# Four sums of a chunk's transform as adding transfers between on-chip tiles

## The chip, the cores and the metric

The kernel runs on one core of one Trainium2 chip. The metric is the device time of one execution in microseconds (us). TensorE multiplies matrices into PSUM banks; VectorE (DVE), ScalarE (ACT) and GpSimd (POOL) work on tiles in SBUF; SyncE (SP) issues the transfers (DMAs), which run on 16 engines that all queues share. Each engine works through its own list of instructions in order and waits on semaphores for the others.

## The reference

Two layers, each a Fourier mixing of a [2048, 512] activation followed by a token-shift and MLP block:

```
def _A_ref(x, dft_seq_re, dft_seq_im, dft_hid_re, dft_hid_im):
    a = jnp.einsum("bsd,ed->bse", x, dft_hid_re)
    b = jnp.einsum("bsd,ed->bse", x, dft_hid_im)
    y = jnp.einsum("ts,bse->bte", dft_seq_re, a) - jnp.einsum("ts,bse->bte", dft_seq_im, b)
    return y
...
x = x + _A_ref(_layernorm(x), ...)
x = x + _B_ref(_layernorm(x), w1, w2, w3, w4)
x = x + _A_ref(_layernorm(x), ...)
x = x + _B_ref(_layernorm(x), w1, w2, w3, w4)
```

`_B_ref` is a layer norm, a product with `w1`, a gelu, shifts of a quarter of the columns by one or two rows, a product with `w2` and a residual, then a second layer norm and an MLP of width 1376. Only the Fourier mixing is touched by the change.

## The kernel before

**Precision.** Every fp32 product is made of three: a matrix is held as a high part, which is its cast to the type `float32r`, and a low part, the rest. `mm3` (lines 294 to 296) issues high x high, high x low and low x high. So each tile that TensorE is to read needs two steps first: a cast on ACT (`high`, line 438, or the ring's line 240) and a subtraction on DVE (`low`, line 441, or the ring's line 257).

**The transform of a chunk.** The 2048 positions are cut into four chunks of 512. The transform along the sequence is done first, on the normalised activation, in two phases of eight steps each: `x_phase` and `y_phase`. Each step takes pieces of the matrices out of a ring of four buffers, which SP's loads, ACT's casts and DVE's subtractions keep filled up to three pieces ahead of TensorE (`stream`, `prefetch`). The phases leave partial products in PSUM, and the real and imaginary parts of the result, each in two halves, come out of them by additions: four tiles `re0`, `im0`, `re1`, `im1` of 128 x 1024 elements, called `rr00`, `rr10`, `rr01`, `rr11` in the profile (with an f where they are written in full precision).

**The product along the hidden dimension.** The four tiles are the stationary side of a second product with the hidden matrices (`hid`, PSUM bank `psd`). For the chunks before the last it is spread over the *next* chunk's `x_phase`: `im0` is used before step 2, `re1` and then `im1` before step 3, `re0` before step 4, and once more each in the later steps. So the sums that finish a chunk run while TensorE is already at work on the next.

**The order around the change.** Nothing is scheduled automatically: each engine's list is in the order of the Python code. The sums that are not needed at once are put into a table `late`; `x_phase` runs entry 2k after it has taken the first piece of step k, and entry 2k + 1 after the second (`run_late`). Before the change the entries 1 to 6 held the additions together with the `high` and `low` of each tile:

```
if c < NC - 1:
    for i, names in enumerate((["im1-"], ["re1+"], ["im1+", "re1"], ["re0+", "im1"], ["re0++"], ["re0"])):
        late[i + 1] = [f for n in names for f in late.pop(n)]
```

Four of these additions take an operand out of `tmp`, where ACT has put the last PSUM results of `y_phase` (lines 544 and 546) and, in its last third, called `X1`, an earlier one (line 535): `re1 += t[0:2]`, `im1 += X1`, `re0 += t[0:2]`, `re0 += t[2:4]`. All additions on DVE are recorded in one helper at line 480. `y_phase` runs for seven chunks (the very first chunk has a phase of its own), and for five of these the code above applies. The last chunk of each layer keeps its own order.

`X1` is also the place into which SP loads the residual rows of the chunk before (line 205), in step 2 of the next `x_phase`; that load has to wait until `X1` has been added.

## Time and profile before

| | before |
|---|---|
| median of 3 runs (lowest to highest) | 1423.1 us (1422.88 to 1423.29) |
| span of the profiled execution, first to last instruction | 1421.1 us |
| DVE busy | 1187.0 us (84%), 1675 instructions |
| ACT busy | 743.0 us (52%) |
| POOL busy | 77.7 us (5%), 105 instructions |
| transfers, all issued by SP | 306.31 MB, mean 216 GB/s |
| clock granted to TensorE | 1.000 on average |

The page's own execution took 1421.1 us from first to last instruction. POOL does almost nothing: it raises to a power for the layer norms (lines 313 and 334) and issues no transfer. A busy share says how long an engine had an instruction in flight; whether that engine sets the end has to be read from the waits of TensorE.

### The profile page before, as it was taken

What the parts mean: (1) busy time and instruction counts of PE and PEld (TensorE: products, weight loads), DVE (VectorE), ACT (ScalarE), POOL (GpSimd) and SP (SyncE); (2) the same over time, 40 slices, a digit from 0 to 9 for tenths busy, and PEclk for the clock granted to TensorE, in tenths of its full rate; (3) what the DMA queues carried; (4) which work ended last, traced back from release to release, by engine and by line L of the source; (5) the groups of instructions that cost most, each with busy time, mean ns of one, the idle gap of its engine ahead of it and who ended that gap; (6) DMA issues with size and microseconds to landing.
All of it is one profiled execution on the core that took longest, in us unless ns stands there. A gap on an engine that the chain in (4) does not pass through costs nothing.

```text
span 1421.1 us, 17861 instructions
## 1 busy us (share of the span) xinstructions
PE 1415.4 (100%) x6465; PEld 1180.1 (83%) x6465; DVE 1187.0 (84%) x1675; ACT 743.0 (52%) x1007; POOL 77.7 (5%) x105
## 2 busy tenths in 40 slices
PE   9999999999999999999999999999999999999998
PEld 7888888888888888888888888888888888899887
DVE  7986998988979888656789989889899788896676
ACT  6663464455566754434555544554555566453351
POOL 2100000000002000000000000000000020000000
PEclk9999999999999999999999999999999999999999
DMA  7867647659754857945556476575696456676864
GB/s 253 279 208 234 210 152 262 193 163 309 238 164 109 294 195 266 354 159 178 196 174 222 152 253 212 158 265 176 193 304 229 134 148 237 202 244 228 311 207 158
DMA packets 136488, 306.31 MB, mean 216 GB/s; under 512 B 9680, under 2 KB 58064, under 8 KB 133712
## 3 DMA queue, kind: packets, MB, share of 16 engines
q1 hardware_dynamic: 136400, 305.17, 65.1%
q8 instruction: 51, 0.84, 0.2%
q14 instruction: 37, 0.30, 0.1%
HBM read 250.87 MB, written 54.26 MB: 215 GB/s over the span
## 4 chain that ended last, share of the span: by engine, by line
PE 93%; DVE 4%; ACT 1%; issue 1%; POOL 0%; DMA 0%; DVEq 0%; ACTq 0%; POOLq 0%
PE psd L294 10%; PE psd L296 10%; PE psd L295 9%; PE psa L296 8%; PE psa L294 8%; PE psa L295 8%; PE psb L296 7%; PE psc L295 7%; PE psc L296 7%; PE psb L294 7%; PE psb L295 7%; PE psc L294 7%; DVE rest L480 0%; ACT tmp L342 0%; DVE ring L257 0%
## 5 line engine op out<-in xcount | busy, mean ns | idle before, releaser
L240 ACT CAST ring<-raw 128x1024 fp32r<-128x1024 f32 x127 | 133.3, 1054 | 78.5 <-PE psd L296 42.9
L257 DVE TENSOR_TENSOR ring<-raw,ring 128x1024 fp32r<-128x1024 f32 x126 | 153.5, 1220 | 13.1 <-ACT ring L240 13.0
L294 PE MATMUL psd<-ring,rr 128*128 128x512 f32 x208 | 80.9, 389 | 0.0
L295 PE MATMUL psd<-ring,rr 128*128 128x512 f32 x208 | 80.9, 389 | 0.0
L296 PE MATMUL psd<-ring,rr 128*128 128x512 f32 x208 | 80.9, 389 | 0.0
L334 POOL TENSOR_TENSOR rs<-ve,mhalf 128x4 f32<-128x4 f32 x16 | 26.9, 1683 | 723.8 <-DVE nm L333 723.8
L247 ACT CAST ring<-ring0f 128x1024 fp32r<-128x1024 f32 x28 | 29.6, 1057 | 50.7 <-DVE ring0f L246 50.7
L257 DVE TENSOR_TENSOR ring<-ring1f,ring 128x512 fp32r<-128x512 f32 (+1 forms) x56 | 53.3, 952 | 0.7 <-ACT ring L243 0.7
L313 POOL TENSOR_TENSOR rs<-ve,mhalf 128x2 f32<-128x2 f32 (+2 forms) x33 | 28.8, 872 | 415.7 <-DVE nb L312 415.7
L342 ACT ACTIVATE tmp<-xs,nb,rs 128x512 f32<-128x512 f32 x56 | 43.5, 814 | 14.6 <-POOL nb L314 14.6
L294 PE MATMUL psc<-ring,ay 128*128 128x512 f32 x128 | 49.8, 389 | 0.0
L295 PE MATMUL psc<-ring,ay 128*128 128x512 f32 x128 | 49.8, 389 | 0.0
L296 PE MATMUL psc<-ring,ay 128*128 128x512 f32 x128 | 49.8, 389 | 0.0
L294 PE MATMUL psb<-ring,ay 128*128 128x512 f32 x128 | 49.8, 389 | 0.0
L295 PE MATMUL psb<-ring,ay 128*128 128x512 f32 x128 | 49.8, 389 | 0.0
L296 PE MATMUL psb<-ring,ay 128*128 128x512 f32 x128 | 49.8, 389 | 0.0
L294 PE MATMUL psa<-ring,ay 128*128 128x512 f32 x126 | 49.0, 389 | 0.0
L295 PE MATMUL psa<-ring,ay 128*128 128x512 f32 x126 | 49.0, 389 | 0.0
L296 PE MATMUL psa<-ring,ay 128*128 128x512 f32 x126 | 49.0, 389 | 0.0
L294 PE MATMUL psd<-ring,ay 128*128 128x512 f32 x126 | 49.0, 389 | 0.0
L295 PE MATMUL psd<-ring,ay 128*128 128x512 f32 x126 | 49.0, 389 | 0.0
L296 PE MATMUL psd<-ring,ay 128*128 128x512 f32 x126 | 49.0, 389 | 0.0
(826 smaller groups left out, 4494.4 us busy)
## 6 DMA issues: line engine op xcount, KB each, us to landing
raw<-in_ws SPq DMA_DIRECT2D x183, 512.0 KB, 5.1
raw<-in_hs SPq DMA_DIRECT2D x56, 512.0 KB, 3.6
w4r<-w4d SPq DMA_DIRECT2D x44, 512.0 KB, 4.5
w3b<-w3d SPq DMA_DIRECT2D x10, 1792.0 KB, 8.9
w3d<-w3b SPq DMA_DIRECT2D x5, 1792.0 KB, 6.9
x1d<-tmp SPq DMA_DIRECT2D x12, 512.0 KB, 6.4
xs<-x1d SPq DMA_DIRECT2D x12, 512.0 KB, 5.0
w4d<-w4in SPq DMA_DIRECT2D x11, 512.0 KB, 4.7
```

The lines of the kernel that those rows point to most:

```text
L240: nc.scalar.copy(dest[:, a:b, 0], r[0][:, a:b])
L247: nc.scalar.copy(dest[:, :, 0], lo)
L257: nc.vector.tensor_tensor(lo, src, hi.bitcast(F32), op=ALU.subtract)
L294: nc.tensor.matmul(o, lh, rh, start=first, stop=False, skip_group_check=more)
L295: nc.tensor.matmul(o, lh, rl, start=False, stop=False, skip_group_check=more)
L296: nc.tensor.matmul(o, ll, rh, start=False, stop=last, skip_group_check=more)
L313: nc.gpsimd.tensor_tensor(rs[:, :n], ve[:, :n], mhalf[:, 0, :n], op=ALU.pow)
L334: nc.gpsimd.tensor_tensor(rs, ve, mhalf[:, :, :2], op=ALU.pow)
L342: nc.scalar.activation(o, s, AF.Identity, bias=mr[2], scale=mr[1])
```

## The change

At the five chunk ends the four additions that read `tmp` leave DVE. POOL issues each as a transfer from `tmp` to the tile that adds to what is there. The first goes out at the end of `y_phase`, the second in entry 0 of the next `x_phase`, the other two in entry 1, after a subtraction `im1 -= re1` that stays on DVE. The `high` and `low` steps of the tiles move to entries 4 to 7. The two additions into `re0` write the same tile, so the second waits for the first to land.

```
+    ident = at("ident", 4 * AY, P, dtype=F32)
+    make_identity(nc, ident)
     for i in range(WARM):
         nc.tensor.matmul(PD[1][:, :P], ident, ident, start=True, stop=True)
...
+    def add_dma(o, a):
+        nc.gpsimd.dma_start(o, a, accum_op=ALU.add)
...
         if c < NC - 1:
-            for i, names in enumerate((["im1-"], ["re1+"], ["im1+", "re1"], ["re0+", "im1"], ["re0++"], ["re0"])):
-                late[i + 1] = [f for n in names for f in late.pop(n)]
+            late.clear()
+            add_dma(re0s, t[:, 0:2])
+            late[0] = [lambda: add_dma(re0s, t[:, 2:4])]
+            late[1] = [
+                lambda: add(im1s, im1s, re1s, ALU.subtract),
+                lambda: add_dma(re1s, t[:, 0:2]),
+                lambda: add_dma(im1s, X1),
+            ]
+            late[4] = [lambda: high(re1), lambda: high(im1)]
+            late[5] = [lambda: low(re1), lambda: low(im1)]
+            late[6] = [lambda: high(re0)]
+            late[7] = [lambda: low(re0)]
...
-    nc = bacc.Bacc("TRN2", target_bir_lowering=False, num_devices=1, dynamic_dma_scratch_size=512)
+    nc = bacc.Bacc("TRN2", target_bir_lowering=False, num_devices=1, dynamic_dma_scratch_size=1024)
```

The last line doubles the SBUF set aside for POOL's transfer descriptors; to make room, the identity matrix of the warm-up products moves from a pool of its own into the kernel's arena (the first lines).

The instructions on ACT at the first changed chunk end, from the copies out of PSUM to the casts of `re1` (`rr_164`, in the change `rr_159`) and `im1` (`rr_166`, `rr_161`). Before:

```order
L546 COPY tmp<-psa_251 128x512
L243 CAST ring_182<-ring3f 128x512
L240 CAST ring_176<-raw_184 128x2x512
L240 CAST ring_178<-raw_185 128x2x512
L438 CAST rr_164<-rr01f 128x2x512
L243 CAST ring_180<-ring2f 128x512
L438 CAST rr_166<-rr11f 128x2x512
L240 CAST ring_182<-raw_186 128x2x512
L240 CAST ring_176<-raw_187 128x2x512
L240 CAST ring_178<-raw_184 128x2x512
```

In the change:

```order
L549 COPY tmp<-psa_246 128x512
L243 CAST ring_177<-ring3f 128x512
L240 CAST ring_171<-raw_179 128x2x512
L240 CAST ring_173<-raw_180 128x2x512
L243 CAST ring_175<-ring2f 128x512
L240 CAST ring_177<-raw_181 128x2x512
L240 CAST ring_171<-raw_182 128x2x512
L438 CAST rr_159<-rr01f 128x2x512
L438 CAST rr_161<-rr11f 128x2x512
L240 CAST ring_173<-raw_179 128x2x512
```

Both casts now stand behind two more casts of ring pieces, with one ring piece (`ring_173` here, `ring_178` before) behind them.

DVE in the same stretch, from the subtraction `im1 -= re1`, with the additions of line 480 and the subtractions of line 441. Before:

```order
L480 TENSOR_TENSOR rr11f<-rr11f,rr01f 128x2x512
L257 TENSOR_TENSOR ring_176<-raw_184,ring_176 128x2x512
L480 TENSOR_TENSOR rr01f<-rr01f,tmp 128x2x512
L242 TENSOR_TENSOR ring2f<-raw_185 128x512
L257 TENSOR_TENSOR ring_178<-raw_185,ring_178 128x2x512
L480 TENSOR_TENSOR rr11f<-rr11f,tmp 128x2x512
L441 TENSOR_TENSOR rr_164<-rr01f,rr_164 128x2x512
L257 TENSOR_TENSOR ring_180<-ring2f,ring_180 128x512
L257 TENSOR_TENSOR ring_182<-raw_186,ring_182 128x2x512
L480 TENSOR_TENSOR rr00f<-rr00f,tmp 128x2x512
L441 TENSOR_TENSOR rr_166<-rr11f,rr_166 128x2x512
```

In the change:

```order
L480 TENSOR_TENSOR rr11f<-rr11f,rr01f 128x2x512
L257 TENSOR_TENSOR ring_171<-raw_179,ring_171 128x2x512
L242 TENSOR_TENSOR ring2f<-raw_180 128x512
L257 TENSOR_TENSOR ring_173<-raw_180,ring_173 128x2x512
L257 TENSOR_TENSOR ring_175<-ring2f,ring_175 128x512
L257 TENSOR_TENSOR ring_177<-raw_181,ring_177 128x2x512
L257 TENSOR_TENSOR ring_171<-raw_182,ring_171 128x2x512
L441 TENSOR_TENSOR rr_159<-rr01f,rr_159 128x2x512
L441 TENSOR_TENSOR rr_161<-rr11f,rr_161 128x2x512
L242 TENSOR_TENSOR ring2f<-raw_179 128x512
```

The additions are gone, and both subtractions stand behind all ring work of the pieces up to the two hidden matrices.

POOL, which had no transfers, has four between the powers of two layer norms (the first row with x2 is the pair that adds into `re0`):

```order
L335 TENSOR_TENSOR nb<-nm,rs 128x4
L483 DMA rr00f<-tmp 128x2x512 x2
L483 DMA rr01f<-tmp 128x2x512
L483 DMA rr11f<-tmp 128x2x512
L334 TENSOR_TENSOR rs<-ve,mhalf 128x4
```

They stand in one list, so while the second transfer into `re0` waits for the first, those for `re1` and `im1` wait with it.

More of the change, by code (lines that the diff above doesn't have):

```diff
@@ L50, in spectral_mlp_kernel @@
     ctx.enter_context(tc.manual_schedule())
-    ident = const.tile([P, P], F32, name="ident")
-    make_identity(nc, ident)
     mhalf = const.tile([P, 2, TC], F32, name="mhalf")
```

## The prediction

> **What bounds the kernel now.** I read the page's first part, then what TensorE (PE) waits for, then the chain of waits, then one changed chunk end in the timeline.

> ```profile
> span 1421.1 us, 17861 instructions
> PE 1415.4 (100%) x6465; PEld 1180.1 (83%) x6465; DVE 1187.0 (84%) x1675; ACT 743.0 (52%) x1007; POOL 77.7 (5%) x105
> PE 93%; DVE 4%; ACT 1%; issue 1%; POOL 0%; DMA 0%; DVEq 0%; ACTq 0%; POOLq 0%
> ```

> A busy PE alone proves little, since the ends of matmuls are modelled. But the list of all that PE waited for has two entries, both in the first microseconds:

> ```profile
> PE psd L139 <- POOL mhalf L55: 1.4, 1, 1.4
> PE psb L426 <- DVE rr L339: 0.2, 1, 0.2
> ```

> So the kernel is a nearly unbroken row of matmuls. The chain gives DVE 4%, and in order of time that DVE share is not at the chunk ends: it runs from the first to the second row below (the start of the second layer), and from the third to the fourth.

> ```profile
> 686.97 0.69 DVE rest L480
> ...
> 739.10 0.50 PE psc L295
> ...
> 1215.34 0.70 DVE rest L480
> ...
> 1244.22 0.50 PE psd L294
> ```

> The five changed ends lie elsewhere (near 192, 290, 799, 897 and 995 us). They have the same pattern; I work on the first, where the next chunk starts at 191.63. Stretches of 4 us from there (PE, PEld, DVE, ACT, POOL, then clock, DMA share and GB/s):

> ```profile
> 191.00:195.00 4.00, 4.00 (x19) 3.33 (x18) 3.17 (x4) 2.36 (x5) 0.00 (x0) 1.00 0.25 76
> 195.00:199.00 4.00, 4.00 (x19) 3.31 (x18) 3.13 (x4) 2.63 (x3) 0.00 (x0) 1.00 0.54 193
> 199.00:203.00 4.00, 4.00 (x20) 3.30 (x19) 4.00 (x5) 2.13 (x4) 0.00 (x0) 1.00 0.86 308
> 203.00:207.00 4.00, 4.00 (x19) 3.34 (x18) 3.66 (x4) 2.64 (x3) 0.00 (x0) 1.00 0.27 68
> ```

> PE is full in each. DVE is nearly full too, but PE never waits for it here. Nothing that takes work off DVE at this place can therefore shorten anything; only something late can lengthen it.

> **What is removed: worth nothing.** By the groups of line 480, the removed additions are 20:

> ```profile
> L480 DVE TENSOR_TENSOR rr00f<-rr00f,tmp 128x1024 f32<-128x1024 f32 x10 | 12.2, 1219 | 0.0
> L480 DVE TENSOR_TENSOR rr11f<-rr11f,tmp 128x1024 f32<-128x1024 f32 x7 | 8.5, 1218 | 0.0
> L480 DVE TENSOR_TENSOR rr01f<-rr01f,tmp 128x1024 f32<-128x1024 f32 x5 | 6.1, 1219 | 0.0
> ```

> 10 + 5 + 5 of the 7 (two belong to the last chunks), 1.22 us each, 24.4 us of DVE. Matmuls cover them all, so the term is 0.

> **The head: 0.** The identity and `mhalf` change places on POOL, same instructions, at this point:

> ```profile
> 1.25 0.10 POOL L55 MEMSET mhalf<- 128x8 f32 x1
> 4.84 0.56 POOL L313 TENSOR_TENSOR rs<-ve,mhalf 128x1 f32<-128x1 f32 x1 [3.48 <-DVE nb L312]
> ```

> The next POOL work waits 3.48 us for DVE, so an order within the first 1.4 us decides nothing.

> **The deadlines.** What the change adds is a wait: `high` of `re1` and `im1` wait for transfers. The first matmuls that read `re1`:

> ```profile
> 206.59 0.39 PE L294 MATMUL psd<-ring,rr 128*128 128x512 f32 x1
> ...
> 209.31 0.39 PE L294 MATMUL psd<-ring,rr 128*128 128x512 f32 x1
> ```

> One hidden product is 12 matmuls at 0.227 us, so `im1` is read from 209.31. Before the change the two tiles were made in time by these steps (the first is `im1 -= re1`, which stays):

> ```profile
> 194.17 1.22 DVE L480 TENSOR_TENSOR rr11f<-rr11f,rr01f 128x1024 f32<-128x1024 f32 x1
> ...
> 196.82 1.22 DVE L480 TENSOR_TENSOR rr01f<-rr01f,tmp 128x1024 f32<-128x1024 f32 x1
> ...
> 200.37 1.22 DVE L480 TENSOR_TENSOR rr11f<-rr11f,tmp 128x1024 f32<-128x1024 f32 x1
> 201.51 1.22 DVE L441 TENSOR_TENSOR rr<-rr01f,rr 128x1024 fp32r<-128x1024 f32 x1
> ...
> 205.95 1.22 DVE L441 TENSOR_TENSOR rr<-rr11f,rr 128x1024 fp32r<-128x1024 f32 x1
> ```

> `re1` was whole at 202.73 (3.9 us early), `im1` at 207.17 (2.1 us early). ACT's rows:

> ```profile
> 190.11 1.06 ACT L544 COPY tmp<-psb 128x512 f32<-128x512 f32 x2
> 191.15 1.27 ACT L546 COPY tmp<-psa 128x512 f32<-128x512 f32 x2
> ...
> 201.63 1.06 ACT L438 CAST rr<-rr11f 128x1024 fp32r<-128x1024 f32 x1 [1.59 <-DVE rr11f L480]
> 202.59 2.00 ACT L240 CAST ring<-raw 128x1024 fp32r<-128x1024 f32 x2
> 205.47 1.06 ACT L240 CAST ring<-raw 128x1024 fp32r<-128x1024 f32 x1 [0.89 <-ACT ring L240]
> ...
> 216.35 1.05 ACT L240 CAST ring<-raw 128x1024 fp32r<-128x1024 f32 x1
> ```

> Once landed, a tile needs a cast (1.06) and a subtraction (1.22), 2.28 us. So `re1` must have landed by 206.59 - 2.28 = 204.3 and `im1` by 209.31 - 2.28 = 207.0. Even with both landed long before, ACT reaches the cast of `re1` only behind the two ring casts that end at 204.59 at the latest (they can run about 1 us earlier without the `im1` cast ahead of them); the places alone leave some half a microsecond, no more. While ACT stands there, one ring cast stands behind it (at 205.47 before), for the piece of step 3, which TensorE reads 24 matmuls behind 206.59, at 212.0; that and the piece's own subtraction leave some 4 us of cover. `re0`, first read at 216.11 by the same count (12 + 12 matmuls and step 3 behind 206.59), has some 10 us more than `re1`, and no deadline of its own.

> **When do the transfers land?** No row shows an adding transfer, nor any that POOL issues. The first (A, into `re0`) can go at 191.2, when ACT's copy (190.11 + 1.06) is done. The second (B) waits for A to land; C (`re1`) and D (`im1`) stand behind B in POOL's list. The nearest rows (KB, then median us to landing):

> ```profile
> raw<-in_hs SPq DMA_DIRECT2D x56, 512.0 KB, 3.6
> zt0f<-zd SPq DMA_DIRECT2D x4, 1024.0 KB, 6.3
> out<-tmp SPq DMA_DIRECT2D x5, 256.0 KB, 2.0
> ```

> For the rate: the stretch 199 to 203 moved 308 GB/s at a share of 0.86, so 358 GB/s when all engines work, and 512 KB take 1.5 us of them. An addition must fetch what lies in the destination as well as the source: 1 MB in, 3.0 us. Lower bound: as a plain 512 KB load, 3.6 us with 1.5 of engine time. Upper bound: as a 1 MB load, 6.3 us with 3.0. I take 3.0 of engine time, because both operands must be read, with a fixed part of 2.0 - 0.75 = 1.25 from the 256 KB row, whose transfers run at the kernel's quiet end: 4.25 us alone.

> [...]

> They share the 16 engines with SP's loads. At this place:

> ```profile
> 196.93 0.33 SPq L222 DMA_DIRECT2D raw<-in_ws  x1
> 197.31 0.43 SPq L1671 DMA_DIRECT2D w4raw<-in_w  x1
> 200.48 0.33 SPq L222 DMA_DIRECT2D raw<-in_hs  x1
> ...
> 205.30 0.43 SPq L205 DMA_DIRECT2D tmp<-in_x  x1
> 208.33 3.20 SPq L222 DMA_DIRECT2D raw<-in_hs  x2
> ```

> Three loads, 4.5 us of engine time, fall among B, C and D.

> - Taken values: A lands 191.2 + 4.25 = 195.4. C's data is through at 195.4 + 1.25 + 6.0 + 4.5 = 207.2, D's at 210.2. PE waits 207.2 - 204.3 = 2.9 us for `re1`, in all 210.2 - 207.0 = **3.2 us** by `im1`. Five ends: 16 us.
> - Lower bound: A 194.8; C and D cannot go before 195.4 either (DVE's subtraction, 194.17 + 1.22), and land at 195.4 + 3.6 + 1.5 + 3.0 = 203.5 and 205.0 with all of two loads ahead. No wait: 0.
> - Upper bound: A 197.5; C 197.5 + 3.3 + 6.0 + 4.5 = 211.3, D 214.3: 7.3 us, five times 36 us.

> So the wait only goes away if a transfer takes well under 4 us alone. PE has no idle time later to win it back.

> **SP's queue.** The load into `X1` (205.30) now waits for D instead of DVE's addition, and what is queued behind it waits too: with D at 210.2 the ring load that went out at 208.33 goes 2 us later. Its cast is the one at 216.35 and it takes 3.6 us to land, so that is covered up to a D at about 212. POOL's next power waits for this sum, long after D has been issued:

> ```profile
> 218.35 1.37 DVE L480 TENSOR_TENSOR tmp<-psd,tmp 128x512 f32<-128x512 f32 x2 [0.97 <-PE psd L296]
> ```

> **Sum.** 0 + 0 + 16 = 16 us: a span of 1437.1. The runs lie 2.0 us above the span (1423.1 against 1421.1), so **1439 us**.

> **The rivals.**

> 1. *The transfers land in time* (same, 1423). The point is 204.3 for C and 207.0 for D. For it: the first stretch shows a DMA share of only 0.25, and the lower bound passes both. Against it: four transfers of which two are strictly one behind the other, and a share of 0.86 just when C and D move. If so, PE waits at most tenths of a microsecond per end for the tight places: 1422.5 to 1425.9.
> 2. *One at a time, or a colder PE* (much slower). The room for POOL's descriptors was doubled only, and if it holds one transfer, C and D each start after the one ahead has landed: D at 195.4 + 3 x 4.25 + 4.5 = 212.7, 5.7 us per end, 1452. A wait could also cost clock: if PE ran at half speed for as long as it had waited, 3.2 us, it would lose 1.6 more per end, 8 us, 1447. The trace grants 1.00 throughout and has no such pause, so it can't tell. [...]
> 3. *DVE's free time is worth something* (faster). The 24.4 us would have to show in waits of PE for DVE at the five ends, and there are none. Time: no better than 1422.

> **Chances.** Forecast (0.6 to 5.4 us per end, 1426 to 1450) 0.5; rival 1 0.36; rival 2 and whatever else lies above 1450, 0.11; rival 3 0.03. A measurement tells 0.2%, 2.8 us, from no change. Faster 0.03; same 0.36; slower 0.61. The range is 1422 to 1456: it takes in rival 1 and the serial transfers of rival 2, and leaves out the far end, where all goes by the upper bound (1459). The forecast's own range is 1426 to 1450.

> **What would show it.** Right: 20 fewer additions on line 480; ACT's line 438 waiting for a transfer at each of the five ends; PE's list of waits with `psd` behind DVE's line 441, five times about 3 us; the adding transfers about 4 us from issue to landing for A, more for C and D. Wrong: no such entry for PE and a landing of C before 204.3; or a wait that is somewhere else, at the ring's casts behind ACT or behind SP's held load.

## The result, and the profile after

The changed kernel takes **1483.5 us** (median of 4 runs, 1482.0 to 1485.4) against 1423.0 us before: a ratio of 1.0426 with a 95% interval of 1.0414 to 1.0438. The forecast was 1439 us with a range of 1422 to 1456. The direction was right; the 60 us are nearly four times the 16 us of the sum.

The first part of the page after, and its row of POOL's transfers (packets, MB, share of the 16 engines' time):

```profile
span 1480.2 us, 17907 instructions
PE 1432.5 (97%) x6465; PEld 1185.4 (80%) x6465; DVE 1165.3 (79%) x1655; ACT 741.9 (50%) x1007; POOL 102.9 (7%) x125
q0 software_dynamic: 5440, 10.49, 4.1%
PE 88%; issue 5%; DMA 4%; DVE 1%; ACT 1%; POOL 1%; POOLq 0%; DVEq 0%
```

DVE has lost its 20 additions and is busy 21.7 us less (1187.0 to 1165.3), and nothing came of it. DMA, which had no share of the chain of waits, now has 4%. The first two rows of the list of all that PE waited for, after (us in total, times, the longest):

```profile
PE psd L294 <- ACT rr L438: 33.9, 6, 7.4
PE psd L296 <- DVE rr L441: 8.3, 10, 1.2
```

The first row is the cast of `re1`, five times 5 to 7 us, and one short wait for the cast of `im1`. The prediction had named `psd` behind DVE's line 441, five times about 3 us; but the first matmul of a product reads the high part alone, so the long wait shows behind ACT's line 438. The second row has two kinds of waits for a low part, of `im1` and of `re0`.

The first changed end in time (start, duration, engine, line, what; in brackets the idle time before and what ended it). POOL's timeline after, the issues A, B, C and D:

```profile
191.38 1.40 POOL L483 DMA_DIRECT2D rr00f<-tmp  x1 [25.88 <-ACT tmp L547]
198.36 1.23 POOL L483 DMA_DIRECT2D rr00f<-tmp  x1 [5.57 <-DMA rr00f<-tmp]
205.79 1.21 POOL L483 DMA_DIRECT2D rr01f<-tmp  x1 [6.20 <-DVE ring L257]
211.00 1.23 POOL L483 DMA_DIRECT2D rr11f<-tmp  x1 [4.00 <-issue]
```

SP's timeline after, the loads around them and the held one into `X1`:

```profile
188.68 5.21 SPq L222 DMA_DIRECT2D raw<-in_hs  x2
196.81 0.33 SPq L222 DMA_DIRECT2D raw<-in_ws  x1
197.19 0.43 SPq L1684 DMA_DIRECT2D w4raw<-in_w  x1
200.36 0.33 SPq L222 DMA_DIRECT2D raw<-in_hs  x1
202.25 0.33 SPq L222 DMA_DIRECT2D raw<-in_ws  x1
215.94 0.38 SPq L205 DMA_DIRECT2D tmp<-in_x  x1
```

ACT's timeline after, the casts of `re1` and `im1`:

```profile
210.70 1.04 ACT L438 CAST rr<-rr01f 128x1024 fp32r<-128x1024 f32 x1 [7.01 <-DMA rr01f<-tmp]
215.95 1.04 ACT L438 CAST rr<-rr11f 128x1024 fp32r<-128x1024 f32 x1 [4.21 <-DMA rr11f<-tmp]
```

The program lets C go as soon as DVE's subtraction and B's issue are done, yet C is issued at 205.79, when B is through, and D at 211.00, right behind C's landing at 210.70. No semaphore asks for that: the transfers go one at a time. (C's row names a ring subtraction of DVE as what ended its wait; it is not that, since in `x1_room` below C goes 0.7 us behind B with the same semaphores.) D lands at 215.94, when SP's held load into `X1` starts; forecast was 210.2.

What the five ends lost can be read off the starts of successive matmuls: undisturbed they are 0.2275 us apart, and what exceeds this adds up to 58.8 us at the five ends, against 59.1 us between the two spans. 34.3 us is the gap before `re1`'s first product (5.3 us in the first end, 6.6 to 7.6 in the others), 7.0 us is a gap of 1.6 at `re0`'s low part in every end, and the rest, 17.5 us, are small waits and matmuls that start 0.43 us apart behind the wait. PE's timeline after:

```profile
206.24 0.39 PE L296 MATMUL psa<-ring,ax 128*128 128x512 f32 x1
211.79 0.80 PE L294 MATMUL psd<-ring,rr 128*128 128x512 f32 x1 [5.16 <-ACT rr L438]
...
214.50 0.63 PE L296 MATMUL psd<-ring,rr 128*128 128x512 f32 x1
214.93 0.63 PE L294 MATMUL psd<-ring,rr 128*128 128x512 f32 x1
...
218.31 0.50 PE L296 MATMUL psd<-ring,rr 128*128 128x512 f32 x1 [0.36 <-DVE rr L441]
```

and by stretches (busy time of PE, PEld, DVE, ACT, POOL, then clock, DMA share, GB/s):

```profile
206.30:211.80 5.50, 0.34 (x3) 0.01 (x1) 0.02 (x1) 1.04 (x1) 1.50 (x2) 0.86 0.59 118
211.80:214.00 2.20, 2.16 (x4) 1.32 (x5) 1.20 (x1) 0.00 (x0) 0.42 (x1) 0.50 0.62 114
214.00:217.00 3.00, 3.00 (x8) 2.31 (x7) 0.00 (x0) 1.05 (x2) 0.00 (x0) 0.50 0.53 94
```

The clock falls to 0.50 within the wait (its mean there is 0.86) and stays there behind it. But PE still has to wait for `im1` at 218.31, so in this end the slow matmuls only fill time before D. In one sum: undisturbed, `im1`'s product would start 13 matmuls behind the one at 206.24, so at 209.2, and needs cast and subtraction, 2.28 us, ahead of it. D is due at 206.9 and lands at 215.94, 9.0 us late; the end loses 8.9 us, `re0`'s gap apart. The same holds in the other four ends (D 10.2 to 11.2 us late, 10.1 to 11.1 lost). **In this run, how late D lands is nearly the whole loss.** It is not the only thing in the way: C is 6.5 us late by the same count in the first end, and `x1_room` shows what C and the slow clock cost when D comes earlier.

### The profile page after: what moved, and what is told of

Its sections match the earlier page's. It is cut to its first block, busy times and chain, and to the rows that moved or that the text cites. A ratio compares the mean times of both kernels' runs of the same rounds, so it can differ in the third digit from the quotient of the medians.

```text
span 1480.2 us, 17907 instructions
## 1 busy us (share of the span) xinstructions
PE 1432.5 (97%) x6465; PEld 1185.4 (80%) x6465; DVE 1165.3 (79%) x1655; ACT 741.9 (50%) x1007; POOL 102.9 (7%) x125
## 3 DMA queue, kind: packets, MB, share of 16 engines
q0 software_dynamic: 5440, 10.49, 4.1%
## 4 chain that ended last, share of the span: by engine, by line
PE 88%; issue 5%; DMA 4%; DVE 1%; ACT 1%; POOL 1%; POOLq 0%; DVEq 0%
PE psd L296 9%; PE psd L294 9%; PE psd L295 9%; PE psa L294 7%; PE psa L295 7%; PE psa L296 7%; PE psc L295 6%; PE psc L294 6%; PE psc L296 6%; PE psb L296 6%; PE psb L294 6%; PE psb L295 6%; DMA rr00f<-tmp 2%; DMA rr11f<-tmp 2%; DVE rr L441 1%
## 5 line engine op out<-in xcount | busy, mean ns | idle before, releaser
L240 ACT CAST ring<-raw 128x1024 fp32r<-128x1024 f32 x127 | 133.6, 1053 | 92.1 <-PE psd L296 59.1
L294 PE MATMUL psd<-ring,rr 128*128 128x512 f32 x208 | 86.2, 415 | 33.9 <-ACT rr L438 33.9
L296 PE MATMUL psd<-ring,rr 128*128 128x512 f32 x208 | 86.4, 415 | 8.5 <-DVE rr L441 8.3
L295 PE MATMUL psd<-ring,rr 128*128 128x512 f32 x208 | 84.9, 408 | 0.0
L294 PEld LDWEIGHTS psd<-ring,rr 128*128 128x128 f32 x208 | 41.7, 200 | 44.9 <-ACT rr L438 36.9
L296 PEld LDWEIGHTS psd<-ring,rr 128*128 128x128 f32 x208 | 41.2, 198 | 24.7 <-DVE rr L441 16.4
L313 POOL TENSOR_TENSOR rs<-ve,mhalf 128x2 f32<-128x2 f32 (+2 forms) x33 | 29.1, 882 | 414.6 <-DVE nb L312 414.6
L342 ACT ACTIVATE tmp<-xs,nb,rs 128x512 f32<-128x512 f32 x56 | 43.3, 810 | 14.4 <-POOL nb L314 13.2
L294 PE MATMUL psc<-ring,ay 128*128 128x512 f32 x128 | 49.8, 389 | 0.0
L296 PE MATMUL psc<-ring,ay 128*128 128x512 f32 x128 | 49.8, 389 | 0.0
L295 PE MATMUL psc<-ring,ay 128*128 128x512 f32 x128 | 49.8, 389 | 0.0
L294 PE MATMUL psb<-ring,ay 128*128 128x512 f32 x128 | 49.8, 389 | 0.0
L295 PE MATMUL psb<-ring,ay 128*128 128x512 f32 x128 | 49.8, 389 | 0.0
L296 PE MATMUL psb<-ring,ay 128*128 128x512 f32 x128 | 49.8, 389 | 0.0
L295 PE MATMUL psa<-ring,ay 128*128 128x512 f32 x126 | 49.0, 389 | 0.0
L296 PE MATMUL psa<-ring,ay 128*128 128x512 f32 x126 | 49.0, 389 | 0.0
L294 PE MATMUL psa<-ring,ay 128*128 128x512 f32 x126 | 49.0, 389 | 0.0
L294 PE MATMUL psd<-ring,ay 128*128 128x512 f32 x126 | 49.0, 389 | 0.0
## 6 DMA issues: line engine op xcount, KB each, us to landing
raw<-in_ws SPq DMA_DIRECT2D x183, 512.0 KB, 5.3
raw<-in_hs SPq DMA_DIRECT2D x56, 512.0 KB, 4.0
w4r<-w4d SPq DMA_DIRECT2D x44, 512.0 KB, 4.7
x1d<-tmp SPq DMA_DIRECT2D x12, 512.0 KB, 6.2
xs<-x1d SPq DMA_DIRECT2D x12, 512.0 KB, 5.0
w4d<-w4in SPq DMA_DIRECT2D x11, 512.0 KB, 4.7
```

Source lines behind the costliest of these rows:

```text
L240: nc.scalar.copy(dest[:, a:b, 0], r[0][:, a:b])
L294: nc.tensor.matmul(o, lh, rh, start=first, stop=False, skip_group_check=more)
L295: nc.tensor.matmul(o, lh, rl, start=False, stop=False, skip_group_check=more)
L296: nc.tensor.matmul(o, ll, rh, start=False, stop=last, skip_group_check=more)
L313: nc.gpsimd.tensor_tensor(rs[:, :n], ve[:, :n], mhalf[:, 0, :n], op=ALU.pow)
L342: nc.scalar.activation(o, s, AF.Identity, bias=mr[2], scale=mr[1])
```

## The experiments

The theory: the transfers go one at a time, for want of room for their descriptors, and SP's loads hold them up. Its rivals: the clock's fall behind the wait costs most; the new places of casts and subtractions cost by themselves; an addition by a transfer is too long whatever its turn. The diffs are against the changed kernel, unless said otherwise, and "..." stands for lines left out. How late D lands at the first end is worked out as above.

### Room for two transfers (x1_room)

```
-...dynamic_dma_scratch_size=1024)
+...dynamic_dma_scratch_size=1536)
```

The SBUF space for it comes from fewer buffers for the small tiles of the layer norms.

> The change with 1536 instead of 1024 bytes per partition for the descriptors of POOL's transfers (and, to make room, fewer buffers for the layer norms' small tiles). Theory A (the room for descriptors lets only one adding transfer be under way, so C waits for B and D for C): now two fit, C is issued within 1.5 us of B at the first end (199.6 to 200 instead of 205.8), D when B has landed; C lands 2 to 4 us earlier, and the time falls from 1483 to 1465 to 1477. Rival theory B (POOL's transfers go one at a time whatever the room): C is still issued only when B has landed, and the time stays at 1483 within 2 us.

Measured: 1474.5 us (ratio to before 1.0367, 1.0350 to 1.0385), 9 us less than the change. POOL's timeline in `x1_room`, C and D:

```profile
199.28 1.73 POOL L483 DMA_DIRECT2D rr01f<-tmp  x1
208.60 1.21 POOL L483 DMA_DIRECT2D rr11f<-tmp  x1 [7.59 <-issue]
```

C now goes right behind B, and D when B has landed: the room did make it one at a time, and with half as much again it is two. But C's median from issue to landing grows from 4.9 to 13.2 us, with B and the loads beside it, and its cast starts at 211.90 in place of 210.70; it was expected 2 to 4 us earlier, so the time came out in its window and this step did not. D lands at 214.44, 7.2 us behind its time in this run, and yet the end loses 9.3 us: now no product waits for `im1`, and what exceeds is C's lateness and the slow clock (0.50 from 211.8 to 218.6). The turns are real, and only a part.

### Only the two transfers into `re0` (x2_re0_only)

```
             add_dma(re0s, t[:, 0:2])
             late[0] = [lambda: add_dma(re0s, t[:, 2:4])]
-            late[1] = [ ...im1 -= re1, add_dma re1, add_dma im1... ]
...
+            late[1] = [lambda: add(im1s, im1s, re1s, ALU.subtract)]
+            late[2] = [lambda: add(re1s, re1s, t[:, 0:2]), lambda: high(re1)]
+            late[3] = [lambda: add(im1s, im1s, X1), lambda: high(im1), lambda: low(re1)]
+            late[4] = [lambda: low(im1)]
+            late[5] = [lambda: high(re0)]
+            late[6] = [lambda: low(re0)]
```

> Only the two sums into re0 are adding transfers (A and B); re1 and im1 are added by DVE, and all casts and subtractions stand at the entries of before. Theory A (the loss is transfers that are too late for their reader): B lands near 205, the cast of re0 comes at 209.5 at the earliest, no wait of PE; 1423 within 1 us. Rival theory C (adding transfers slow the ring's loads, or POOL's writing of descriptors slows DVE, so that the loss comes with the transfers themselves): half of the transfers, so a good part of the 60 us, 1440 or more, without waits for line 441 or 438.

Measured: 1423.1 us (ratio 1.0001, 0.9992 to 1.0011), no wait of PE at the five ends. B landed at 208.5 and not near 205, still in time. Two adding transfers at each end, ten additions less on DVE in all: no loss, and no gain either. What DVE is spared is worth nothing here, and transfers that are in time cost nothing.

### The places alone (x3_places)

```
...
+            late[1] = [lambda: add(im1s, im1s, re1s, ALU.subtract), lambda: add(re1s, re1s, t[:, 0:2])]
+            late[2] = [lambda: add(im1s, im1s, X1), lambda: add(re0s, re0s, t[:, 0:2])]
+            late[3] = [lambda: add(re0s, re0s, t[:, 2:4])]
             late[4] = [lambda: high(re1), lambda: high(im1)]
```

No transfers at all; the rest of the table as in the change.

> No adding transfer: all additions on DVE, early (entries 1 to 3), but casts and subtractions at the entries 4 to 7 of the change. Theory A (the subtraction of re0 stands behind two ring steps of DVE that wait for PE to finish half a step, so the place alone costs 1.4 us per end, and the places of re1 and im1 cost nothing): 1423 + 5 x 1.4 = 1430, with PE waiting for line 441 five times. Rival (the places cost nothing as long as the data is there, and the wait for re0 in the change is only a consequence of the stall before it): 1423 to 1425.

Measured: 1431.0 us (ratio 1.0056, 1.0041 to 1.0071). `re1` and `im1` are in time; at `re0`, PE's timeline of `x3_places` shows, here in the first of five ends alike,

```profile
216.24 0.39 PE L295 MATMUL psd<-ring,rr 128*128 128x512 f32 x1
217.87 0.50 PE L296 MATMUL psd<-ring,rr 128*128 128x512 f32 x1 [1.24 <-DVE rr L441]
```

a gap of 1.63 us, 1.40 more than usual. DVE's timeline of the change tells why:

```profile
223.67 0.69 DVE L242 TENSOR_TENSOR ring1f<-raw 128x512 f32<-128x512 f32 x1 [1.89 <-PE psb L296]
224.28 1.22 DVE L257 TENSOR_TENSOR ring<-raw,ring 128x1024 fp32r<-128x1024 f32 x1
225.41 1.22 DVE L441 TENSOR_TENSOR rr<-rr00f,rr 128x1024 fp32r<-128x1024 f32 x1
```

In entry 7 `re0`'s subtraction stands behind two ring subtractions, the first of which waits for PE itself to free a piece. So it comes late however early `re0` is whole. This is 8 of the 60 us, and has nothing to do with transfers.

### `re0`'s steps back where they were (x6_re0_early)

```
-            late[5] = [lambda: low(re1), lambda: low(im1)]
-            late[6] = [lambda: high(re0)]
-            late[7] = [lambda: low(re0)]
+            late[5] = [lambda: low(re1), lambda: low(im1), lambda: high(re0)]
+            late[6] = [lambda: low(re0)]
```

> The change as it is, but re0's cast and subtraction are back one step of the list each (5 and 6, as before the change). Theory (the place of re0's low part, behind two ring subtractions that wait for PE's own pieces, costs 1.6 us per end by itself): no pause of 1.6 us at re0's first matmul, 8 us less, 1475 us. Rival (the pause only hides in what the ends lose anyway, or re0's cast then waits for something else): within 2 us of the change, 1482 to 1485 us.

Measured: 1475.4 us (ratio 1.0370, 1.0355 to 1.0385), 8.1 us less than the change, as the theory had it. The term stands by itself. D's lateness is 10.2 to 11.7 us in the five ends of this run, and the ends lose 9.9 to 11.5: D sets them here too.

### Keeping PE warm (x5_warm)

```
...
+                if h == 1 and keep["on"]:
+                    for _ in range(44):
+                        nc.tensor.matmul(PD[0][:, :P], s[:, 0, 0, :P], zero, start=False, stop=False)
...
```

44 products with a matrix of zeros, 128 columns each, stand ahead of `re1`'s first product and add nothing to the sum.

> The change, with 44 extra matmuls of 128 columns ahead of the first product with re1 at each of the five ends; they multiply by a tile of zeros and add nothing to psd, and fill about 5 us of PE's wait (room for the zeros from the small tiles' buffers). Theory D (PE's clock drops while it waits 5 to 8 us, and the next dozen matmuls run at 0.43 instead of 0.23 us): the spacing stays at 0.23 behind the wait, 2 to 3 us per end less, 1483 - 10 to 15 = 1468 to 1473. Rival theory E (the slow dozen is slow because its operands or the transfers beside it are): same slow spacing, 1483 or a little more.

Measured: 1487.8 us (ratio 1.0451, 1.0436 to 1.0467), so 4 us more. `x5_warm` by stretches (columns as above):

```profile
206.60:211.80 5.20, 5.20 (x47) 5.12 (x45) 0.00 (x0) 0.00 (x0) 1.21 (x1) 1.00 0.30 88
211.80:215.40 3.60, 0.20 (x2) 0.06 (x1) 0.00 (x0) 1.03 (x1) 0.73 (x1) 1.00 0.63 113
215.40:217.00 1.60, 1.34 (x3) 0.61 (x4) 1.23 (x1) 0.01 (x1) 0.49 (x1) 0.59 0.38 69
```

The clock held through the zero products. It fell in the pause behind them (3.7 us in this end, 2.3 to 3.1 in the others) or up to 0.6 us after it, so the matmuls behind the wait were slow all the same, and the time is nearer the rival's than the theory's. C was issued at 209.45 here and D landed at 219.61, 12.2 us late in place of 9.0; in the other ends D is 10.7 to 11.7 us late. Why B took longer in the first end is not settled. A warm PE could not have helped while D sets the end, so this run tells nothing on the price of the clock.

### Without the two into `re0` (x4_re1_im1), and with room for two (x11_re1_im1_room)

```
-            add_dma(re0s, t[:, 0:2])
-            late[0] = [lambda: add_dma(re0s, t[:, 2:4])]
...
+            late[2] = [lambda: add(re0s, re0s, t[:, 0:2])]
+            late[3] = [lambda: add(re0s, re0s, t[:, 2:4])]
             late[4] = [lambda: high(re1), lambda: high(im1)]
...
+            late[5] = [lambda: low(re1), lambda: low(im1), lambda: high(re0)]
+            late[6] = [lambda: low(re0)]
```

> Only C (into re1) and D (into im1) are transfers; both sums into re0 are DVE's again, and re0's cast and subtraction stand where they stood before the change. Theory (the transfers are late because each stands behind the ones ahead of it, and the two into re0 go first): C goes at 195.4, right behind DVE's subtraction, and lands by 200 to 202, D by 206 to 208.5; deadlines 204.3 and 207.0: PE waits 0 to 1.5 us per end, 1423 to 1431 us. Rival (an adding transfer at this place is too slow whatever its order, since the three ring loads are served ahead of it): C lands behind 207 or D behind 211, 4 us or more per end, 1443 us or more.

> As x4_re1_im1 (only C and D are transfers), with room for two transfers. Theory (in x4_re1_im1 D was late because it went only when C had landed, at 205.3): D goes 1 to 2 us behind C, lands by 207 to 209, PE waits 0 to 1.5 us per end, 1423 to 1431 us. Rival (the three ring loads hold both, and two at once only share what is left): D lands at 210 or later, 1440 us or more.

Measured: 1444.3 us (ratio 1.0149, 1.0134 to 1.0164) and 1433.6 us (ratio 1.0074, 1.0056 to 1.0092). POOL's timeline in `x4_re1_im1`:

```profile
196.17 1.40 POOL L483 DMA_DIRECT2D rr01f<-tmp  x1 [30.39 <-ACT ring L240]
205.35 1.23 POOL L483 DMA_DIRECT2D rr11f<-tmp  x1 [7.78 <-issue]
```

and in `x11_re1_im1_room`:

```profile
195.81 1.39 POOL L483 DMA_DIRECT2D rr01f<-tmp  x1 [30.40 <-ACT ring L240]
196.73 1.72 POOL L483 DMA_DIRECT2D rr11f<-tmp  x1
```

`x4_re1_im1` was a miss for the theory, and its time is the rival's: C, alone and 9.6 us earlier, took 8.8 us (median) in place of 4.9, because now it was C that had the loads beside it, and D had to wait for it: landed 210.81, 3.6 us late. With room for both, D lands at 209.15, 2.3 us late, and the time falls by 10.7 us, somewhat short of what was expected. Being first does not bring D in time while it has to wait for C's turn.

### Another order (x7_order), and all mends at once (x10_all)

```
             add_dma(re0s, t[:, 0:2])
-            late[0] = [lambda: add_dma(re0s, t[:, 2:4])]
             late[1] = [
                 lambda: add(im1s, im1s, re1s, ALU.subtract),
                 lambda: add_dma(re1s, t[:, 0:2]),
                 lambda: add_dma(im1s, X1),
+                lambda: add_dma(re0s, t[:, 2:4]),
             ]
```

`x10_all` is this order, with the room of `x1_room` and the places of `x6_re0_early`.

> The four transfers in the order A, C, D, B, all else as in the change: the second one into re0 goes last. Theory (one at a time, the order decides what is late): C is issued at 198.4, where B was, and lands 7 to 10 us later as B did; D is issued then and lands 5 us later. PE waits 1.5 to 4.5 us for re1 and about as much in all by im1 plus tenths; with re0's place (8 us) 1448 to 1463 us. Rival (C's landing is set by the ring loads and not by B): the wait for re1 stays at 5 us or more, 1475 us or more.

> All three mends in one, all four transfers still there: room for two transfers (as in x1_room), the order A, C, D, B, and re0's cast and subtraction at 5 and 6. Theory (the three costs are separate): C goes right behind A at 195.4 and lands by 203 to 206, D by 209 to 211; PE waits 0 to 4 us per end in all, 1425 to 1443 us. Rival (the loads ahead hold C as long as before): 5 us or more per end, 1450 us or more.

Measured: 1466.6 us (ratio 1.0317, 1.0299 to 1.0335; the four runs spread from 1461.8 to 1471.2), 16.9 us less than the change and just over the expected window; and 1438.6 us (ratio 1.0105, 1.0087 to 1.0123), 44.9 us less, inside its window. The three mends alone came to 9.0 + 16.9 + 8.1 = 34 us. In `x7_order` the second transfer into `re0`, now last, is late itself: PE waits up to 1.1 us more at `re0` than by its place alone. Even with all three mends, the four transfers leave 15.6 us of loss.

### Copies in place of additions (x9_copy), and copies one at a time (x13_copy_one)

```
-        nc.gpsimd.dma_start(o, a, accum_op=ALU.add)
+        nc.gpsimd.dma_start(o, a)
```

In `x13_copy_one` the room for descriptors is 512 in place of 1024 as well. Both leave the four sums out.

> The four transfers only copy (the destination is overwritten, the sums into re0, re1 and im1 are left out); bytes written, places and waits as in the change. This prices the second read of an addition. Theory (each transfer takes 1.4 us less, 3.5 in place of 4.9 alone, and three stand ahead of the last): 4 to 6 us per end less, 1450 to 1465 us. Rival (the turns and the loads ahead set the time, whatever a transfer reads): 2 us per end less at most, 1473 us or more.

> As x9_copy (the four transfers only copy, the sums are left out), with half the room for POOL's descriptors (512 in place of 1024). In x9_copy a copy went in 144 packets (2880 in 20 transfers) against the addition's 272 (5440 in 20), and B, C and D were issued 0.7 us behind each other, so the turns were gone as well as the second read. Theory (the turns are the larger part): with half the room copies go one at a time again, C is issued when B has landed, and PE waits 2 to 5 us at re1 or im1 in each end, 1443 to 1465 us. Rival (the second read, that is the length of each transfer, is what costs): copies that go one at a time still land in time, within 4 us of x9_copy, 1428 to 1436 us.

Measured: 1431.4 us (ratio 1.0058, 1.0042 to 1.0074) and 1445.7 us (ratio 1.0164, 1.0147 to 1.0181). The page's row of POOL's queue in `x9_copy`:

```profile
q0 software_dynamic: 2880, 10.49, 2.0%
```

POOL's timeline in it, B, C and D:

```profile
196.58 0.73 POOL L483 DMA_DIRECT2D rr00f<-tmp  x1 [3.93 <-DMA rr00f<-tmp]
197.31 0.72 POOL L483 DMA_DIRECT2D rr01f<-tmp  x1
198.03 0.73 POOL L483 DMA_DIRECT2D rr11f<-tmp  x1
```

and in `x13_copy_one`, with half the room:

```profile
196.47 0.74 POOL L483 DMA_DIRECT2D rr00f<-tmp  x1 [4.18 <-DMA rr00f<-tmp]
202.98 0.72 POOL L483 DMA_DIRECT2D rr01f<-tmp  x1 [5.76 <-DVE ring L257]
209.57 0.73 POOL L483 DMA_DIRECT2D rr11f<-tmp  x1 [5.87 <-issue]
```

Copies of the same bytes at the same places lose hardly more than `re0`'s place costs (8.4 against 8.1 us). The gain was far above what was expected: a copy also goes in 2880 / 20 = 144 packets against 5440 / 20 = 272, so that the same room took B, C and D at once. With half the room the turns come back and cost 14.3 us; additions in place of copies, in turns, cost another 37.8. **Of these two steps the length of an addition is the larger, and its packets make the turns on top.** The expectation of `x13_copy_one` had its time right and took the turns for the larger part. The split goes by this order of steps: a turn costs what the transfer in it lasts, so the two are not separate terms, and four additions with room for all were not run. The share of the queue prices it: 0.041 x 1480.2 us / 20 = 3.0 us of all 16 engines for an addition, 0.020 x 1430.4 / 20 = 1.4 us for a copy.

### Less of SP's loads (x12_thin)

Four ring loads around each end fetch 16 of the 128 partitions, and the kernel leaves out the rest of these pieces.

```
-            nc.sync.dma_start(raws[i][:, a:b], src)
+            p = 16 if state["thin"] else P
+            state["thin"] = max(0, state["thin"] - 1)
+            nc.sync.dma_start(raws[i][:p, a:b], src[:p])
...
+            state["thin"] = 4
```

> The change as it is, but four of the ring loads around each of the five ends fetch only 16 of 128 partitions (64 KB in place of 512 KB; the rest of these pieces is left stale, so the products of these pieces are left out in effect). One load of 512 KB stays among B and C. Theory (the loads are served ahead of queued adding transfers): B and C each take 5 to 6 us in place of 7 to 10, the wait for re1 falls to 1 to 4 us, 1445 to 1466 us. Rival (an adding transfer and its turn take this long by themselves): the wait for re1 falls by 1 us at most, 1476 us or more.

Measured: 1467.7 us (ratio 1.0314, 1.0298 to 1.0331), 15.8 us less, just over the expected window. B's turn in the second end, issue to issue, by POOL's timeline of the change:

```profile
305.87 1.22 POOL L483 DMA_DIRECT2D rr00f<-tmp  x1 [4.87 <-DMA rr00f<-tmp]
315.33 1.21 POOL L483 DMA_DIRECT2D rr01f<-tmp  x1 [8.24 <-issue]
```

and of `x12_thin`:

```profile
304.23 1.22 POOL L485 DMA_DIRECT2D rr00f<-tmp  x1 [5.13 <-DMA rr00f<-tmp]
310.89 1.21 POOL L485 DMA_DIRECT2D rr01f<-tmp  x1 [5.45 <-issue]
```

9.5 us against 6.7, and D's turn, beside which no load ran, 4.9 in both. Beside B three loads were cut by 448 KB each, 3.8 us at the 358 GB/s that the prediction worked out, so B's turn got back some three quarters of what the loads beside it take. D is 7.1 to 8.0 us late in this run, and the ends lose 7.0 to 7.9 besides `re0`'s place.

### When the clock falls (x8_delay, x14_pause)

`x8_delay` is the kernel before, with ACT's cast of `re1` repeated 6, 7, 8, 10 and 13 times in the five ends; `x14_pause` is `x3_places` with it 3, 4, 5, 6 and 8 times. Neither has a transfer of POOL's. The edit of the second; the first makes the same of `high(re1)` in the entry `"re1+"`:

```
-late[4] = [lambda: high(re1), lambda: high(im1)]
+late[4] = [lambda: high(re1)] * next(ends) + [lambda: high(im1)]
```

> The kernel before, without any transfer, but ACT's cast of re1 is made 6, 7, 8, 10 and 13 times in the five ends (same values each time), 1.05 us each: this gives PE pauses of 0 to 6 us that have nothing to do with transfers. What is asked is when the granted clock falls. [...] If in the change the clock fell for another reason (the load of the transfers, the weak pieces around), it stays at 1.00 in all five. Time by the pauses alone: 1423 + about 10 to 16 us, 2 to 3 us more for each end with a drop.

> x3_places (no transfers, the change's places) with ACT's cast of re1 made 3, 4, 5, 6 and 8 times in the five ends (same values). By x3_places' rows the cast would end at 204.58, and 1 us later for each repeat, with 2.0 us of slack and subtraction to the first matmul at 206.6: single pauses of 1.2, 2.2, 3.2, 4.2 and 6.2 us. If the clock falls with the length of one pause, it stays 1.00 in the first two ends and falls in the last two, and the third is at the edge. If a fall goes by where the pause lies in a fixed grid of 3.4 us, the second may fall and the third or fourth stay. Time 1431 + 17 us of pauses + 2 to 3 us for each fall, 1450 to 1460 us.

Measured, one run each: 1452.4 and 1454.6 us. In `x8_delay` the repeats held up the ring's casts too, so each pause came in two pieces; the clock stayed up in the first two ends (2.1 us and less in all) and fell in the other three. In `x14_pause` the single pauses are 0.4, 1.5, 2.5, 3.6 and 5.8 us, each but the last followed by one of 0.7 for `im1`; matmuls 0.43 us apart follow in the last three ends. Its stretches in the third end, through the pause and behind it:

```profile
820.00:823.00 3.00, 0.62 (x4) 0.20 (x2) 0.11 (x1) 2.94 (x4) 0.00 (x0) 1.00 0.80 270
823.00:824.50 1.50, 0.97 (x3) 0.54 (x4) 1.50 (x2) 1.50 (x2) 0.00 (x0) 0.90 0.99 397
824.50:827.00 2.50, 2.50 (x7) 1.95 (x7) 2.50 (x4) 0.87 (x2) 0.00 (x0) 0.50 0.07 30
```

So the fall belongs to the pause and not to the transfers. It came after 2.5 us of pause, and costs 1.9, 1.9 and 3.4 us in the three ends.

```profile
208.25:211.66 3.41, 1.83 (x8) 1.13 (x6) 0.00 (x0) 0.84 (x1) 0.00 (x0) 1.00 0.52 93
...
310.66:314.07 3.41, 1.49 (x6) 0.71 (x5) 1.74 (x2) 2.81 (x3) 0.00 (x0) 1.00 0.54 105
314.07:317.48 3.41, 3.41 (x10) 2.64 (x9) 3.41 (x5) 1.70 (x3) 0.00 (x0) 0.50 0.86 284
```

The first, with a pause of 2.0 us that ends in the next window, is 0.48 full and the clock holds; the second, with pauses of 1.6 and 0.7 us both inside, is 0.28 full and the clock falls at its end. (The busy time that the view gives is longer, since it counts each matmul to its modelled end.)

## Why the prediction went wrong

The failing step is the landing of C and D: "C's data is through at 195.4 + 1.25 + 6.0 + 4.5 = 207.2, D's at 210.2". It let B, C and D share the engines without a gap, and D landed at 215.94. By its own steps:

| | forecast | measured, first end |
|---|---|---|
| A lands | 195.4 | 197.8 |
| an addition alone | 4.25 us (3.0 of it engines) | 4.9 us (3.0 of it engines) |
| A landed to D landed | 14.8 us | 18.2 us (20.2 to 21.2 in the others) |
| D late | 3.2 us | 9.0 us (11 in the third and fourth end) |
| `re0` | "no deadline of its own" | 1.4 us in every end |
| clock | 1.00 | 0.50 behind every wait |

- **Turns.** Rival 2 had this mechanism and its price: three turns of 4.25 and the loads, 17.25 us from A to D, against 18.2 measured in the first end and 20.2 to 21.2 in the others. It had a chance of 0.11, with the rest above 1450. By measured terms, three transfers alone are 14.7 us, POOL's delays between a landing and the next issue (0.3 to 0.65 each) 1.2 to 1.3, and the rest, 2.3 to 5.3, is what B takes longer beside the loads (7.2 to 10.2 us in place of 4.9). What decided it was in the change itself, the room for descriptors, but how many packets an addition needs no row of before could tell. `x1_room` and `x13_copy_one` show the turns.
- **A.** Taken to run alone, it landed 2.4 us later than forecast in the first end. 0.65 us of this is the longer transfer. The second ring load of the row that stands at 188.68 (x2, 5.21 us) went out about 193.6, in the middle of A: in `x12_thin`, where that load is cut to 64 KB, A takes 5.4 us in place of 6.4. In the other ends of the change A took 5.4 to 5.5 with such a load beside it. The prediction quoted loads behind A and missed this one.
- **The loads.** The prediction counted three loads among B, C and D. The profile before has a fourth, between the rows that it shows:

```profile
204.92 0.33 SPq L222 DMA_DIRECT2D raw<-in_ws  x1
```

In the change this load goes out at 202.25, beside B. It follows a ring subtraction of DVE that ended at 204.90 before and at 202.23 in the change, since DVE no longer has the additions ahead of it: the relieved engine sent a load into the transfers earlier.

- **Engine time.** The 3.0 us for an addition was right: 3.0 by the queue's share, 3.0 / 1.4 = 2.1 times a copy's 1.4. In the trace it shows as twice the data packets at half the size (256 of 2 KB for an addition, 128 of 4 KB for a copy), each of which takes about as long (187 and 177 ns). That it is because both operands are read was the author's argument: no run tells a second read from the smaller packets.
- **`re0`.** "Some 10 us more ... and no deadline of its own" looked at when the tile is whole and not at what its subtraction stands behind: 7 us in the five ends (`x3_places`, `x6_re0_early`).
- **The clock.** It fell in all five ends, and was not in the sum. In the change this cost little of its own: with D as late as it was, PE had to wait for `im1` anyway. It shows as soon as D comes earlier (`x1_room`: 7.2 us late, 9.3 lost).
- **DVE's time: 0.** Right (`x2_re0_only`, for ten of the twenty). **The head and SP's held load: 0.** Right as far as seen: no wait of PE behind the ring's casts or loads in the list after.

With D's lateness of 9.0 to 11.2 us in place of 3.2, and 1.4 for `re0`, the same sum gives 10.4 to 12.6 per end, and the five ends lost 10.3 to 12.5. The upper bound, 7.3 us per end, had A's landing nearly right (197.5) and was too low because it had neither the turns nor the fourth load.

## What to carry to other kernels

Work that was moved from an engine with cover to transfers gained nothing here, where the engine was not waited for (DVE was busy 21.7 us less), and its result came at the time of a queue (D 9.0 to 11.2 us late): sum up the turns, the issue of each, and every load in flight from the first issue to the last landing, also those that the relieved engine will let go earlier, and compare this with the deadline before looking at busy shares. An adding transfer took twice a copy's time on the engines here (3.0 us against 1.4) and nearly twice its packets (272 against 144), so the room for descriptors that held three copies (1024) held one addition. Where a step moves in a list, look at what it stands behind there, and not only at when its input is ready.

## What was not expected of the hardware

- An addition of 512 KB between SBUF tiles took 272 packets and a copy 144. One copy but not two fit a room of 512, three copies or one addition a room of 1024, two additions a room of 1536. All of this fits a room of half as many packets as the number set (256, 512, 768), which is an estimate worked out from these counts and not measured; a room that holds four additions was not run.
- An addition alone took 4.9 us from issue to landing, of which POOL's issue is 1.2; with two in flight beside loads, C took 13.2 in the median (`x1_room`).
- In `x14_pause` the clock fell to half after single pauses of PE of 2.5 us and more, and not after 1.5 us. In `x4_re1_im1` a pause of 2.0 us was followed by no slow matmul in two ends and by some in two others, and one of 1.6 us by seven, so the length alone does not decide. What went with the fall in these traces is how full a window of 3.413 us was: with at most 0.39 the clock fell, with at least 0.42 it held.
